# Output projection of a segment recurrence: four column groups of 160 columns against two chunks on two groups of 320 columns each

## The chip, the cores and the metric

The kernel runs on one core of one Trainium2 chip. A core has a TensorE (PE in the profile; its weight loads are PEld), a VectorE (DVE), a ScalarE (ACT), a GpSimd (POOL), and a SyncE (SP) that in this kernel only issues transfers. The metric is the device time of one execution in microseconds.

## What is computed

Four layers run one after the other on 2048 tokens of width 640: A, B, A, B, each added to its input and each fed with a layer-normed copy of it. Layer A is the one that the change touches. Cut to what matters:

```python
# x: 2048 x 640, 32 heads of 192, segments of 32 tokens, a memory of 8 rows
mem = mem0
for s in range(64):
    h = concat([mem, x[32*s : 32*s+32]])             # 40 x 640
    q, k, v = h @ Wq, h @ Wk, h @ Wv                 # each 40 x 6144
    p = softmax(where(mask, q @ k.T * scale, -1e9))  # per head
    o = (p @ v) @ Wo                                 # 6144 -> 640
    mem = o[:8]                                      # feeds the next segment
    outs.append(o[8:])
```

The first 8 rows of a segment's output are the first 8 rows of the next segment's input. So the 64 segments of a layer A form a chain, and two layers A make 128 segments. Layer B is a linear attention whose work is not a chain; the diff leaves it alone.

## The kernel before

**Stages.** A layer A first projects everything that does not depend on the memory (`A_pre`: the last 8 token rows of every segment, written to DRAM as `kqb` and `vb`). Then `A_chain` walks the segments with the remaining 32 rows (8 memory rows, 24 token rows). The order of instructions in `A_chain` is written out by hand (`tc.manual_schedule()`), one order per engine, as the program emits them.

**Rounds.** The 6144 features are cut into four rounds of 1536, taken forwards in even segments and backwards in odd ones (`rounds`). Here n = 0 to 3 counts the rounds in the order in which they are taken. For each round there are three projections of 20 matmuls (Q, K, V: five pieces of the 640 inputs, each on four column groups of 32 output partitions, 384 columns wide), the scores, the exponential (`weigh`), the sums, the product with V (`attend`), the scaling by the reciprocal into the tile OT (`scale_out`), and the output projection `wo_round`. Rounds overlap: the Q and K of the next round are projected between the scores and the product of this one. The order in the middle of a segment is Q(n+1), sums, attend, scores(n), K(n+1), V(n), `wo_round` of the round before. At the end three `wo_round` calls stand close together, with V(3), sums, attend and scores between and before them.

**wo_round.** A round's OT is 12 chunks of 128 features by 32 rows. For each chunk, four matmuls use the same stationary chunk; column group g gets output columns 160g to 160g+159. All 12 chunks of all four rounds are added up in one PSUM tile, `W`, of 128 partitions by 160 columns: 48 matmuls with 48 weight loads per round, 192 of each per segment.

**From W to the next segment.** After the last `wo_round`, `fill(SEG_FILL)` puts 27 one-column weight loads on PE. VectorE transposes W in two parts (L1161) and casts 8 columns of each block into `hT` (L1162), the transposed input of the next segment; its 24 token rows were put there before by `hx_transpose` (L895) from `xr`. Then PE projects Q of the next segment, first the pieces b = 2, 3, 4, then 0, 1. ScalarE evicts Q (`raw`, L955) and after it copies W to `io` (`keep_rows`, L902), from where POOL stores it to DRAM (`store_rows`, L906).

**The extra rows.** The 8 rows that `A_pre` prepared enter by POOL copies: `next_kq` copies them into QT and KT (L916 to L919) and issues the next load of `kqb` (L910); `place_v` copies rows of V (L930) and issues the next (L926). Their attention output leaves the same way: `store_tail` copies 96 columns of OT to `otb` (L1027) and issues a transfer of it to DRAM (L1028). `otb`, OT, `io`, `raw` and `rc` are single buffers: each new write waits until the last reader, or the transfer, is done. `io` holds the rows that are stored and then the rows that are loaded, so the load of `xr` (L890) waits for the landing of the store.

**POOL's order in one segment.** `store_tail` of the last round of the segment before; `store_rows`; `next_kq(0)`; the load of `xr`; `next_kq(1)`; `store_tail` of round 0; `place_v`; `next_kq(2)`; `store_tail` of round 1; `next_kq(3)`; `store_tail` of round 2; `place_v`. The four copies into `otb` are called copy(0) to copy(3) below, after their rounds.

**Weights.** Three of five pieces of one round of Wq, Wk and Wv and one round of Wo do not fit in SBUF; SP loads them anew in every segment into slots (9 loads' worth of 384 KB and 6 of 320 KB, in all about 5.4 MB), as PE frees the slots.

Of the kernel before, what the change touches and what calls it, by code (L numbers as in the profile page):

```python
# [8 lines left out]
P = 128  # L9
BF16 = mybir.dt.bfloat16  # L10
F32 = mybir.dt.float32
ACT = mybir.ActivationFunctionType
ALU = mybir.AluOpType
# [5 lines left out]
LN_EPS = 1e-5  # L19

FILL = {0: 86, 2: 78}
SEG_FILL = 27

LATE = 64512
ARENA = 202752
# [90 lines left out]
class Kernel:  # L116
# [746 lines left out]
    def A_chain(self, xn_dram, at_dram, li, load_slot, piece, load_wo, late_wo, wo_mid, wo_end, low):  # L863
        nc, tc, KC, NSEG = self.nc, self.tc, self.KC, self.NSEG
        scale = float(self.Dh) ** -0.5
        NR = 4
        with tc.tile_pool(name=f"A{li}_ch", reuse_waits="tile", bufs=1) as sp, \
# [6 lines left out]
            OT = sp.tile([P, 6, 80], BF16, name="OT")  # L874
# [4 lines left out]
            def rounds(s):  # L879
                return range(NR) if s % 2 == 0 else range(NR - 1, -1, -1)  # L880

            def load_rows(s):
                io = sp.tile([P, 160], BF16, name="xr", tag="io")
                if s == 0:
                    for g in range(4):
                        c = slice(160 * g, 160 * g + 160)
                        nc.gpsimd.dma_start(out=io[32 * g:32 * g + 8, :], in_=self.A_mem0[:, c])
                        nc.gpsimd.dma_start(out=io[32 * g + 8:32 * g + 32, :], in_=xn_dram[0:24, c])
                else:
                    nc.gpsimd.dma_start(out=io[:, :],  # L890
                                        in_=xn_dram[32 * s - 8:32 * s + 24, :].rearrange("t (g c) -> g t c", g=4))
                return io
# [4 lines left out]
            def new_hT():  # L897
                return sp.tile([P, KC, 32], BF16, name="hT", tag="hT")

            def keep_rows(W):  # L900
                io = sp.tile([P, 160], BF16, name="orow", tag="io")
                nc.scalar.activation(out=io[:, :], in_=W[:, 0:160], func=ACT.Copy)  # L902
                return io

            def store_rows(s, io):
# [2 lines left out]
            def load_kqb(s, r):  # L908
                kqb = sp.tile([P, 192], BF16, name="kqb", tag="kqb", bufs=2)
                nc.gpsimd.dma_start(out=kqb[:], in_=self.kqb_d[s, :, r, :])  # L910
                return kqb
# [46 lines left out]
            def to_rows(raw, m, r=0):  # L958
                if m == "K":
                    nc.vector.transpose(out=KT[:, :, 0:64], in_=raw.rearrange("p (c j) -> p c j", j=64))  # L960
                else:
                    rv = raw.rearrange("p (x i j) -> p x i j", i=3, j=64)
                    q = 16 * (r % 2)
                    nc.vector.transpose(out=QT[:, :, 0:4:3, q:q + 64], in_=rv[:, :, 0:3:2, :])  # L964
                    nc.vector.transpose(out=QT[0:64, :, 1, q:q + 64], in_=rv[0:64, :, 1, :])
                    nc.vector.transpose(out=QT[64:P, :, 2, q:q + 64], in_=rv[64:P, :, 1, :])
# [63 lines left out]
            def wo_round(W, r, first, last):  # L1030
                m0 = 16 * (r % 2)
                w = wo_end[:, :] if r in (0, 3) else wo_mid[:, 7680 * (r - 1):7680 * r]
                for i in range(12):
                    G, c = (i // 4, i % 4) if i < 8 else (i % 4 // 2, 4 + i % 2)
                    for g in range(4):
                        nc.tensor.matmul(W[32 * g:32 * g + 32, 0:160], lhsT=OT[:, c, m0 + 32 * G:m0 + 32 * G + 32],  # L1036
                                         rhs=w[:, 640 * i + 160 * g:640 * i + 160 * g + 160], start=(first and i == 0),
                                         stop=(last and i == 11), tile_position=(0, 32 * g), skip_group_check=True)

            def fill(n):  # L1040

# [5 lines left out]
            def next_kq(s, n):  # L1047

                at = NR * s + n + 1
                if at < len(turns):  # L1050
                    extra_kq(kqs.pop(0), turns[at][1] % 2)
                    if at + 2 < len(turns):
                        kqs.append(load_kqb(*turns[at + 2]))

            xr = load_rows(0)
# [8 lines left out]
            hT = new_hT()  # L1064
            hx_transpose(hT, xr)
            W = None
            for s in range(NSEG):
                order = rounds(s)
                L = NR - 1

                def q_or_k(m, n):
                    ps = pqp.tile([P, 512], F32, name="ps_qk", tag="qk")
                    project(hT, ps, m, n, s)
                    return to_raw(ps, m == "K" and n == 0)

                def values(n, pool, tag):
                    pv = pool.tile([P, 512], F32, name="ps_v", tag=tag)
                    project(hT, pv, "V", n, s)
                    return pv

                raw = q_or_k("Q", 0)
                if s > 0:
                    io = keep_rows(W)
                to_rows(raw, "Q", order[0])
                if s == 0:
                    fill(FILL[li])
                to_rows(q_or_k("K", 0), "K")
                if s == 0:
                    late_wo(2)
                if s > 0:  # L1090
                    store_rows(s - 1, io)
                W = pop.tile([P, 512], F32, name="ps_w", tag="w")
                raw = q_or_k("Q", 1)
                pv = values(0, pop, "v")
                v_rows(pv, 0, "s")
                v_rows(pv, 1, "s")
                S = scores(order[0])
                to_rows(raw, "Q", order[1])
                next_kq(s, 0)
                E = weigh(S)  # L1100
                to_rows(q_or_k("K", 1), "K")
                if s + 1 < NSEG:
                    xr = load_rows(s + 1)
                for n in range(1, L):
                    raw = q_or_k("Q", n + 1)
                    sums(S, E)
                    O = attend(E)
                    if n == 2:
                        place_v()
                    S1 = scores(order[n])  # L1110
                    rc = reciprocals(S)
                    E = weigh(S1)
                    S = S1
                    to_rows(raw, "Q", order[n + 1])
                    next_kq(s, n)
                    if n == L - 1:
                        to_rows(q_or_k("K", n + 1), "K")
                        scale_out(O, rc)
                    else:
                        rawk = q_or_k("K", n + 1)  # L1120
                        scale_out(O, rc)
                        to_rows(rawk, "K")
                    store_tail(s, order[n - 1])
                    pv = values(n, pop, "v")
                    v_rows(pv, 0, "s")
                    v_rows(pv, 1, "s")
                    if n < L - 1:
                        wo_round(W, order[n - 1], n == 1, False)
                        if n == 1:
                            load_wo(order[L])  # L1130
                            if s == NSEG - 1:
                                load_wo(3, low[:, 0:7680])
                pv = values(L, pqp, "qk")
                sums(S, E)
                O = attend(E)
                S1 = scores(order[L])
                next_kq(s, L)
                rc = reciprocals(S)
                E = weigh(S1)
                v_rows(pv, 1, "v")  # L1140
                v_rows(pv, 0, "s")
                wo_round(W, order[L - 2], False, False)
                sums(S1, E)
                O1 = attend(E)
                if s + 1 < NSEG:
                    hT = new_hT()
                    hx_transpose(hT, xr)
                scale_out(O, rc)
                store_tail(s, order[L - 1])
                if s + 1 < NSEG:  # L1150
                    place_v()
                wo_round(W, order[L - 1], False, False)
                rc = reciprocals(S1)
                scale_out(O1, rc)
                wo_round(W, order[L], False, True)
                store_tail(s, order[L])
                fill(SEG_FILL)
                if s + 1 < NSEG:
                    wt = sp.tile([P, KC, 32], F32, name="wt", tag="raw")
                    for b0, b1 in ((2, 5), (0, 2)):  # L1160
                        nc.vector.transpose(out=wt[:, b0:b1, :], in_=W[:, 0:160].rearrange("p (j b) -> p b j", b=KC)[:, b0:b1, :])  # L1161
                        nc.vector.tensor_copy(out=hT[:, b0:b1, 0:8], in_=wt[:, b0:b1, 0:8])  # L1162
            store_rows(NSEG - 1, keep_rows(W))

    def post_steps(self, ops):
# [69 lines left out]
```

## Time and profile before

| what | value |
|---|---|
| three runs | 4068.06, 4073.5, 4086.9 us (median 4073.5) |
| the profiled execution: time, span | 4067.7 us, 4066.0 us |
| mean granted TensorE clock | 0.937 |
| PE matmul busy, PEld busy | 3463.6 us (85%), 2357.2 us (58%) |
| DVE, ACT, POOL busy | 2025.3, 1939.6, 1959.6 us |
| instructions for PE in the trace | 142,876 |
| HBM read and written | 853.72 MB, 73.40 MB |
| segment to segment, mean of 124 (start of L1161 to start of L1161) | 24.03 us |

The two chains of segments take the stretches from about 214 to 1705 us and from about 2248 to 3737 us, some three quarters of the time. A row of the profile's groups gives line, engine, operation, output and inputs, shape and count, then the busy time in us, the mean of one in ns, and the idle time of the engine just before it with what ended that idle time. "issue" is time in which an engine waited for nothing that the profile shows. The matmul's end is modelled, so the distance between the starts of matmuls is a better measure of pace than their length.

### The profile page before, as it was taken

To read this page: it belongs to the slowest core of one execution; us is meant where nothing else is said; L and a number is where in the kernel's file an instruction comes from. 1 tells how busy PE (TensorE), PEld (TensorE's weight loads), DVE (VectorE), ACT (ScalarE), POOL (GpSimd) and SP (SyncE) were. 2 spreads that over 40 slices of the span, in tenths; PEclk is the share of its full clock that TensorE was granted. 3 is DMA by queue.
4 is the path that set the end of the run, shared out by engine and by line. 5 is a ranking of instruction groups with operands and counts; after the bars stand their busy time and mean duration, and the time that the engine had idled before them with its cause. 6 is when DMAs were issued, how large, how long until landed. Compare 5 with 4: busy or idle time off the path is not lost.

```text
span 4066.0 us, 167638 instructions
## 1 busy us (share of the span) xinstructions
PE 3463.6 (85%) x69290; PEld 2357.2 (58%) x72926; DVE 2025.3 (50%) x5432; ACT 1939.6 (48%) x4389; POOL 1959.6 (48%) x4871
## 2 busy tenths in 40 slices
PE   9988888888888888889899888888888888888898
PEld 6755555555555555555377555555555555555553
DVE  5444445445444555446633444554454544544465
ACT  2344455545545455536433444554454545545363
POOL 3455555555555555530333555555555555555300
PEclk9999999999999999989899999999999999999899
DMA  9977777777777777750377777777777777777400
GB/s 304 315 253 252 246 257 261 253 240 254 257 254 250 246 258 262 264 158 1 133 248 235 265 241 248 264 261 242 243 260 252 260 241 249 262 261 261 153 1 27
DMA packets 531754, 934.60 MB, mean 230 GB/s; under 512 B 145458, under 2 KB 295690, under 8 KB 531002
## 3 DMA queue, kind: packets, MB, share of 16 engines
q1 hardware_dynamic: 428858, 818.87, 58.5%
q0 software_dynamic: 68480, 91.75, 7.4%
q10 hardware_dynamic: 33664, 13.24, 1.3%
q8 instruction: 558, 9.14, 0.9%
q14 instruction: 194, 1.59, 0.1%
HBM read 853.72 MB, written 73.40 MB: 228 GB/s over the span
## 4 chain that ended last, share of the span: by engine, by line
PE 48%; DMA 17%; issue 12%; POOL 7%; DVE 6%; PEld 6%; ACT 3%; POOLq 0%; SPq 0%; DVEq 0%; ACTq 0%
PE ps_qk L947 20%; DMA otb<-otb 13%; PE ps_v L947 5%; PE ps_w L1036 4%; PE ps_pre L825 3%; PE ps_s L985 3%; PEld L1036 2%; PEld L1043 2%; PE ps_o L1010 2%; DVE OT L1022 2%; PE ps_qk L391 2%; PE ps_s L996 2%; POOL otb L1027 2%; PE ps_s L980 1%; DVE OT L1018 1%
## 5 line engine op out<-in xcount | busy, mean ns | idle before, releaser
L947 PE MATMUL ps_qk<-arena,hT 128*32 128x384 bf16 x20480 | 1092.8, 352 | 186.1 <-issue 104.0
L947 PEld LDWEIGHTS <-hT 128*32 128x32 bf16 x30720 | 839.0, 101 | 626.1 <-issue 257.0
L955 ACT ACTIVATE raw<-ps_qk 128x384 bf16<-128x384 f32 x1024 | 503.0, 491 | 1287.6 <-PE ps_qk L947 1135.8
L1036 PE MATMUL ps_w<-arena,OT 128*32 128x160 bf16 x24576 | 572.9, 247 | 159.0 <-DVE OT L1018 150.8
L1036 PEld LDWEIGHTS <-OT 128*32 128x32 bf16 x24576 | 454.0, 102 | 254.1 <-DVE OT L1018 221.2
L964 DVE STREAM_TRANSPOSE QT<-raw 128x256 bf16<-128x256 bf16 x512 | 228.0, 445 | 705.9 <-PE ps_s L985 467.1
L947 PE MATMUL ps_v<-arena,hT 128*32 128x384 bf16 x10240 | 509.3, 327 | 14.0 <-DMA arena<-in_A_Wv_dram 13.8
L972 ACT ACTIVATE Vp<-ps_v 64x384 bf16<-64x384 f32 x896 | 433.5, 484 | 96.8 <-PE ps_v L947 76.4
L960 DVE STREAM_TRANSPOSE KT<-raw 128x384 bf16<-128x384 bf16 x512 | 296.1, 578 | 321.2 <-ACT raw L955 314.8
L1018 DVE TENSOR_TENSOR OT<-ps_o,rc 128x320 bf16<-128x320 f32 x512 | 251.5, 491 | 359.5 <-POOL otb L1027 259.8
L1010 PE MATMUL ps_o<-E,Vp 96*128 96x80 bf16 x4096 | 259.0, 202 | 143.3 <-issue 143.0
L910 POOL DMA_DIRECT2D kqb<-kqb x512 | 288.2, 563 | 163.8 <-POOL KT L919 146.7
L1028 POOL DMA_DIRECT2D otb<-otb x512 | 281.2, 549 | 169.4 <-POOL otb L1027 148.3
L1010 PEld LDWEIGHTS <-Vp 96*128 96x128 bf16 x4096 | 222.9, 99 | 187.1 <-DVE OT L1022 136.5
L1022 DVE TENSOR_TENSOR OT<-ps_o,rc 64x160 bf16<-64x160 f32 x1024 | 324.2, 317 | 13.8
L1027 POOL COPY otb<-OT 128x96 bf16<-128x96 bf16 x512 | 135.6, 265 | 324.5 <-DMA otb<-otb 191.0
L930 POOL COPY Vp<-Vp 32x896 bf16<-32x896 bf16 x256 | 237.1, 926 | 77.8 <-PE ps_o L1010 58.6
L1002 ACT ACTIVATE rc<-ps_s 128x320 f32<-128x320 f32 x512 | 224.0, 437 | 77.6 <-DVE OT L1022 64.9
L1001 ACT ACTIVATE ps_s<-ps_s 128x320 f32<-128x320 f32 x512 | 218.6, 427 | 76.4 <-PE ps_s L996 69.9
L985 PE MATMUL ps_s<-QT,KT 128*96 128x80 bf16 (+1 forms) x3072 | 246.1, 217 | 7.8 <-POOL KT L919 3.4
L985 PEld LDWEIGHTS <-KT 128*96 128x96 bf16 x3072 | 222.1, 125 | 39.2 <-issue 28.3
L916 POOL COPY QT<-kqb 128x64 bf16<-128x64 bf16 x512 | 124.2, 242 | 225.9 <-PE ps_s L985 219.3
(149 smaller groups left out, 4744.4 us busy)
## 6 DMA issues: line engine op xcount, KB each, us to landing
arena<-wo_rows SPq DMA_DIRECT2D x792, 320.0 KB, 6.8
arena<-in_A_Wq_dram SPq DMA_DIRECT2D x427, 384.0 KB, 4.6
arena<-in_A_Wv_dram SPq DMA_DIRECT2D x427, 384.0 KB, 6.3
arena<-in_A_Wk_dram SPq DMA_DIRECT2D x768, 192.0 KB, 5.0
kqb<-kqb POOLq DMA_DIRECT2D x512, 48.0 KB, 5.1
arena<-in_A_Wk_dram SPq DMA_DIRECT2D x43, 384.0 KB, 6.9
vb<-arena POOLq DMA_DIRECT2D x128, 112.0 KB, 5.8
Vp<-vb POOLq DMA_DIRECT2D x256, 56.0 KB, 4.8
```

What stands on the lines that cost most here:

```text
L910: nc.gpsimd.dma_start(out=kqb[:], in_=self.kqb_d[s, :, r, :])
L930: nc.gpsimd.tensor_copy(out=Vs[64:96, :], in_=Vs[96:P, :])
L947: nc.tensor.matmul(ps[32 * g:32 * g + 32, 0:384], lhsT=hT[:, b, :], rhs=rhs, start=(i == 0), stop=(i == KC - 1), tile_position=(0, 32 * g) ...
L955: nc.scalar.activation(out=raw, in_=ps[:, 0:384], func=ACT.Copy)
L960: nc.vector.transpose(out=KT[:, :, 0:64], in_=raw.rearrange("p (c j) -> p c j", j=64))
L972: nc.scalar.activation(out=o, in_=i, func=ACT.Copy)
L985: nc.tensor.matmul(S[0:96, c0:c0 + 80 * (q1 - q0)], lhsT=KT[:, 3 * x + i, :], rhs=QT[:, x, q0:q1, :], start=False, stop=(x == 1 and i == 2 ...
L1010: nc.tensor.matmul(O[:, 80 * c:80 * c + 80], lhsT=Vs[0:96, 448 * x + k:448 * x + k + 128], rhs=E[0:96, 160 * x + 80 * e:160 * x + 80 * e + ...
L1018: nc.vector.tensor_tensor(out=OT[:, 0:4, :], in0=ov[:, 0:4, :], in1=rc[:, :].rearrange("p (c q) -> p c q", q=80), op=ALU.mult)
L1022: nc.vector.tensor_tensor(out=OT[h, 4:6, :], in0=ov[h, 4:6, :], in1=rv[h, :, e, :], op=ALU.mult)
L1028: nc.gpsimd.dma_start(out=self.otb_d[s, :, 96 * r:96 * r + 96], in_=ob[:, :])
L1036: nc.tensor.matmul(W[32 * g:32 * g + 32, 0:160], lhsT=OT[:, c, m0 + 32 * G:m0 + 32 * G + 32], rhs=w[:, 640 * i + 160 * g:640 * i + 160 * g ...
```

## The change

`wo_round` takes two chunks at a time. Column groups 0 and 1 work on chunk j, groups 2 and 3 on chunk j+1; each matmul is 320 columns wide (two strips of 160, by an access pattern over the weights), so that partitions 0 to 63 of W collect the even chunks and 64 to 127 the odd ones, over 320 columns. A round is 24 matmuls of 320 columns in place of 48 of 160. W then holds two halves that must be added: for `hT` the transposes cover both strips, and four additions of 64 partitions take the place of two casts; for the stored rows ScalarE copies each half to the other partitions (`half`), and VectorE adds. `keep_rows` is emitted before the Q projection's eviction, not after it. The load of `xr` moves behind `next_kq(1)`. The 27 one-column weight loads go.

```diff
-SEG_FILL = 27
+SEG_FILL = 0
@@ keep_rows
+                half = sp.tile([P, 160], F32, name="half", tag="raw")
                 io = sp.tile([P, 160], BF16, name="orow", tag="io")
-                nc.scalar.activation(out=io[:, :], in_=W[:, 0:160], func=ACT.Copy)
+                for h in range(2):
+                    a, b = slice(64 * h, 64 * h + 64), slice(64 - 64 * h, 128 - 64 * h)
+                    nc.scalar.activation(out=half[a, :], in_=W[b, 160 * h:160 * h + 160], func=ACT.Copy)
+                for h in range(2):
+                    a = slice(64 * h, 64 * h + 64)
+                    nc.vector.tensor_tensor(out=io[a, :], in0=W[a, 160 * h:160 * h + 160], in1=half[a, :], op=ALU.add)
@@ wo_round
-                for i in range(12):
-                    G, c = (i // 4, i % 4) if i < 8 else (i % 4 // 2, 4 + i % 2)
+                for j in range(0, 12, 2):
                     for g in range(4):
-                        nc.tensor.matmul(W[32 * g:32 * g + 32, 0:160], lhsT=OT[:, c, m0 + 32 * G:m0 + 32 * G + 32],
-                                         rhs=w[:, 640 * i + 160 * g:640 * i + 160 * g + 160], start=(first and i == 0),
-                                         stop=(last and i == 11), tile_position=(0, 32 * g), skip_group_check=True)
+                        i = j + g // 2
+                        G, c = (i // 4, i % 4) if i < 8 else (i % 4 // 2, 4 + i % 2)
+                        wi = w[:, 640 * i:640 * i + 640].rearrange("p (h e c) -> p e h c", h=2, e=2)
+                        nc.tensor.matmul(W[32 * g:32 * g + 32, 0:320], lhsT=OT[:, c, m0 + 32 * G:m0 + 32 * G + 32],
+                                         rhs=wi[:, g % 2], start=(first and j == 0), stop=(last and j == 10),
+                                         tile_position=(0, 32 * g), skip_group_check=True)
@@ A_chain, start of a segment
-                raw = q_or_k("Q", 0)
                 if s > 0:
                     io = keep_rows(W)
+                raw = q_or_k("Q", 0)
...
                 to_rows(q_or_k("K", 1), "K")
-                if s + 1 < NSEG:
-                    xr = load_rows(s + 1)
                 for n in range(1, L):
...
                     next_kq(s, n)
+                    if n == 1 and s + 1 < NSEG:
+                        xr = load_rows(s + 1)
@@ A_chain, end of a segment
-                    wt = sp.tile([P, KC, 32], F32, name="wt", tag="raw")
+                    wt = sp.tile([P, 2, KC, 32], F32, name="wt", tag="rc")
+                    wv = W[:, 0:320].rearrange("p (h j b) -> p h b j", h=2, b=KC)
                     for b0, b1 in ((2, 5), (0, 2)):
-                        nc.vector.transpose(out=wt[:, b0:b1, :], in_=W[:, 0:160].rearrange("p (j b) -> p b j", b=KC)[:, b0:b1, :])
-                        nc.vector.tensor_copy(out=hT[:, b0:b1, 0:8], in_=wt[:, b0:b1, 0:8])
+                        nc.vector.transpose(out=wt[:, :, b0:b1, :], in_=wv[:, :, b0:b1, :])
+                        for h in range(2):
+                            a, b = slice(64 * h, 64 * h + 64), slice(64 - 64 * h, 128 - 64 * h)
+                            nc.vector.tensor_tensor(out=hT[a, b0:b1, 0:8], in0=wt[a, h, b0:b1, 0:8], in1=wt[b, h, b0:b1, 0:8],
+                                                    op=ALU.add)
```

PE's instructions per segment go from 1019 to 800, besides five semaphore waits that stand in both.

## The prediction

> **What bounds the kernel now.** I read the page first, then the waits, then the chain and the timeline of some segments, and at last the same events averaged over 124 segments ("phase" below: us after the start of the first transpose L1161, which follows the end of W; a segment lasts 24.03).
>
> ```profile
> span 4066.0 us, 167638 instructions
> ...
> q8 instruction: 558, 9.14, 0.9%
> ...
> PE 48%; DMA 17%; issue 12%; POOL 7%; DVE 6%; PEld 6%; ACT 3%; POOLq 0%; SPq 0%; DVEq 0%; ACTq 0%
> ...
> L1036 PE MATMUL ps_w<-arena,OT 128*32 128x160 bf16 x24576 | 572.9, 247 | 159.0 <-DVE OT L1018 150.8
> ```
>
> PE has less than half of the chain. 17% is transfers, nearly all of `otb`, and 12% is "issue". Queue q8 fetches instructions: 142,876 PE instructions in 558 packets are 256 a packet.
>
> ```profile
> DVE OT L1018 <- POOL otb L1027: 259.8, 114, 5.1
> PE ps_o L1010 <- issue: 143.0, 121, 2.0
> PE ps_qk L947 <- issue: 104.0, 117, 2.2
> POOL xr L890 <- DMA attn<-orow: 93.0, 73, 3.3
> ```
>
> The second and third rows are one thing. Counted along PE, both gaps stand at the same place modulo 256 in every segment (1019 instructions and 5 semaphore waits make 1024, four packets), and each ends 2.3 to 2.5 us after a q8 packet started. They are waits for instructions: one in K(3), at phase 14, 1.1 us in the mean, one in the last `attend`, at phase 20, 1.3 us. The other two boundaries of a segment cost 0.0 and 0.2. The packet itself starts 3.5 to 3.7 us after the boundary before while weights stream, and about 1 us after it when they don't: while weights stream, 256 instructions can't take less than some 6.2 us.
>
> ```profile
> 1023.16 5.95 DMA otb<-otb
> ...
> 1029.24 0.26 POOL otb L1027
> ...
> 1029.79 2.96 DMA otb<-otb
> ...
> 1032.87 0.27 POOL otb L1027
> ...
> 1035.69 3.55 PE ps_qk L947 x54
> ...
> 1048.32 1.14 issue
> ```
>
> The chain shows the other bound: copy(0), its transfer, copy(1), its transfer, copy(2), then `scale_out` and the last `wo_round`. Mean phases: copy(0) 11.33, landing 17.2; copy(1) 17.7, landing 21.5; copy(2) 21.7; W ends at 24.0. copy(2) is bound by the landing in 100 of 122 segments. That landing comes 0.8 us (median) after the last weight packet, which ends at 20.4 (19.8 to 21.3): the weights, at 330 to 370 GB/s from phase 2.5 to 18, hold it up.
>
> **The change part by part**, per segment; 126 segment ends.
>
> *Matmuls.* In a round the 48 matmuls start over 0.792 us, 16.9 ns apart. [...] PE is paced by columns, 12 x 160 = 6 x 320, so I take 0.
>
> *Instructions.* PE loses 192 for the matmuls and 27 in the fill: 805 a segment, 3.14 packets. [...] The rows show 247 us of stalls, so removing all would be 2.0 us a segment if they were on the path. The boundaries now drift by 37 instructions a segment. The densest stretch (K(2), V(1), `wo_round`, Q(3) to V(3): 320 instructions in some 7.1 us) takes 5.7 us for 256, against 6.2: I allow 0 to 0.5 us in about half of the segments, with slack behind it.
>
> *What the stalls were worth.* K(3)'s 1.1 us: `scale_out` of round 2 ended at 17.17 and now at 16.1. But copy(1) also waits for copy(0)'s landing, 17.21. The moved `xr` load is why that comes earlier: POOL's four copies of `next_kq(1)` start 1.02 us after the scores are done, 0.07 without the load before them. The load (0.71 us of POOL, no gap) then stands between the `kqb` issue and copy(0): scores at 8.30 + 0.07 + 1.01 copies + 0.30 + 0.57 issue + 0.71 = 10.96, so copy(0) gains 0.3, and its landing with it (16.9; its transfer is now right behind `xr`'s, which could cost up to 0.4). Its other neighbours on the queue only change places; the store of 8.27 has landed long before. copy(1): 17.7 to 17.1. copy(1)'s transfer lands earlier by 0.42 of what it is issued earlier (fit over the segments), by all of it if the weights let it, by nothing if not: 0 to 0.6, value 0.45. The last `attend`'s 1.3 us ends in front of `scale_out`'s wait for copy(2); it counts only where the second last `wo_round` came later than copy(2) (44 of 122): 0.13 mean. Sum -0.58.
>
> *W to Q.*
>
> ```profile
> 1035.14 0.28 DVE L1161 STREAM_TRANSPOSE wt<-ps_w 128x96 f32<-128x96 f32 x1 [0.90 <-PE L1043]
> 1035.46 0.17 DVE L1162 CAST hT<-wt 128x24 bf16<-128x24 f32 x1
> 1035.55 0.23 DVE L1161 STREAM_TRANSPOSE wt<-ps_w 128x64 f32<-128x64 f32 x1
> ```
>
> The transpose of 96 columns takes 283 ns, of 64 231: 52 per 32, so 192 take 0.44, +0.16. Two additions in place of the cast, the second starting some 0.1 later: +0.10 (as casts cost 0.19, 64x160 additions 0.32). The second part ends 0.54 after Q starts and is needed after three pieces, 0.48: +0.04. Sum +0.30, straight on the path, and the weight stream starts that much later too.
>
> *keep_rows.* Two ScalarE copies (128x160 took 298 ns) run in its idle time before Q's eviction; two additions of 317 ns (L1022's) on DVE, after `hT`'s, end about 2.0 after W. Q's eviction now waits for them through the buffer of `raw`, and K's, Q(1)'s stand behind it on ACT; it started at 1.59 at the earliest, so with +0.30 at most 0.1 is exposed, and KT had 0.25 in hand before PE's scores. 0; if that cover is gone, 0.1. `wt` in the buffer of `rc` only follows DVE's own reads and K(0)'s eviction later: 0.
>
> *The fill.* It ran in PE's wait for `hT` (0.40 of 0.67 us): 0 by itself. Its part in the clock is next.
>
> *The clock.* The trace grants half clock in pieces of 3.413 us or two of them. Such a piece follows a window of 3.413 us in which matmuls were busy for less than about half (33 drops: 0.17 to 0.55; windows without: tenth percentile 0.68).
>
> ```profile
> 1029.00:1032.40 3.40, 1.38 (x53) 1.00 (x52) 1.04 (x3) 0.44 (x1) 2.19 (x7) 1.00 0.09 29
> 1032.40:1035.80 3.40, 1.50 (x52) 1.53 (x83) 1.65 (x6) 0.00 (x0) 2.26 (x5) 0.76 0.08 22
> 1035.80:1039.20 3.40, 3.40 (x64) 1.87 (x64) 1.34 (x5) 1.18 (x3) 1.51 (x3) 0.73 0.63 197
> ```
>
> 71 of 124 segment ends have one. Those pieces are not idle: the last `wo_round` then takes 1.5 us, not 1.0, and segments whose front was slow lasted 0.4 longer. Now the 1.3 us of the last `attend` move behind the second last `wo_round`, so idle time lies in one stretch of up to 2.9 us. The range is -0.1 (the waits shrink) to +0.8 (nearly every end slow, two pieces each). I take +0.05, because 1.0 of the moved idle time was already in the same window.
>
> Sum: -0.58 + 0.30 + 0.05 = -0.23 us a segment, x 126 = -29 us. The profiled execution took 4067.7 (2 us around its span); the median is 4073.5, 6 above it. 4073.5 - 29 = 4045.
>
> **The rivals.** *The landing follows copy(1) fully and the drops grow rarer:* -0.58 becomes -0.9, the clock gives 0.1 or more back: -0.7 us, about 3985. For it: issue is 12% of the chain. Against: the last weight packet doesn't depend on K(3).
>
> *The change only trades one wait for another:* the landing stays at the last weight packet, 0.13 is left against 0.30: +0.15, 4075 to 4095.
>
> *Slower by the clock:* the merged idle stretch drops the clock at nearly every segment end, and often for two pieces, which the Q, K and V projections then run in. It decides once the window before the last `wo_round` is busy for less than half in over nine of ten ends. Price: last `wo_round` +0.2, front +0.5 (Q(2)'s phase runs from 8.7 to 10.6 with the clock): +0.75 instead of 0.05, sum +0.45, or 4130; with part of it hidden under the weights 4100. For it: the removed fill and stalls; against: copy(1) earlier shortens the wait.
>
> *The change doesn't do what it says:* if the weights' two-strip pattern slows the 320 columns, `wo_round` lasts over 0.85 us; the K projections' own stepped pattern runs at V's pace, so this is unlikely.
>
> **How the numbers follow.** A run tells about 0.5%, 20 us, from nothing. Likeliest case (0.45): 4010 to 4070. Fully following (0.25): 3940 to 4010. Trade (0.12) around 4085; slower by the clock and others (0.18): 4095 to 4130. Faster by over 0.5% (under 4053): 0.25 + 0.32 of 0.45 = 0.57. Within: 0.13 + 0.10 = 0.23. Slower: 0.02 + 0.18 = 0.20. Range 3945 to 4108.
>
> **What the profile after would show.** Right: `wo_round` starts spread over 0.8 us still; PE's "issue" rows for L947 and L1010 fall from 247 to under 60 us; `xr` no longer waits for `attn`; copy(1) near phase 17.3, W-to-Q 0.3 longer; DVE's wait for `otb` stays or grows. Wrong: if "issue" stays, the instruction fetch is misread; if the granted clock falls below 0.92, the clock rival has won; if the last weight packet moves earlier by more than 0.3, something I hold fixed moved.

## The result, and the profile after

| | before | after |
|---|---|---|
| median, lowest and highest of 20 runs, us | 4078.49 (4062.24 to 4098.35) | 4086.76 (4065.58 to 4106.55) |
| ratio after to before, 95% interval | | 1.0019 (1.0001 to 1.0038) |
| the profiled execution, us | 4067.7 | 4097.91 |
| mean granted TensorE clock in it | 0.937 | 0.914 |
| segment to segment, us (mean of 124) | 24.03 | 24.23 |

The forecast was 29 us faster. What came is 8 us slower by the medians, 0.2%, within the 0.5% that a measurement of this kernel tells from nothing. Phases below are mean times after the first transpose of W (L1161 before, L1170 after) in the profiled executions. These two lie 11 us under and 11 us over their medians, so the segments in the table show 0.20 us of loss where the medians make it 0.06. With the change, lines move: `wo_round` is L1044, the projections are L953, `half` is L905, the addition of the stored rows L908, the addition into `hT` L1173, the copies into `otb` L1033. The page after:

```profile
span 4096.2 us, 140384 instructions
...
PE 3500.1 (85%) x57018; PEld 2106.2 (51%) x57182; DVE 2181.2 (53%) x5940; ACT 1981.7 (48%) x4517; POOL 1957.4 (48%) x4871
...
q8 instruction: 448, 7.34, 0.7%
...
L1044 PE MATMUL ps_w<-arena,OT 128*32 128x320 bf16 x12288 | 565.6, 320 | 351.0 <-DVE OT L1024 341.8
...
L905 ACT ACTIVATE half<-ps_w 64x160 f32<-64x160 f32 x256 | 76.3, 298 | 666.4 <-DVE wt L1170 489.7
```

27,000 instructions are gone, and instruction packets fall from 558 to 448. `wo_round` is as busy as before, 565.6 us against 572.9, with half the matmuls. But its idle time in front has gone from 159.0 to 351.0 us. DVE has 156 us more to do. (The chain on this page covers only a few per cent of the span, so it isn't read.) In the waits, PE's "issue" rows for the K projection and `attend` are gone; counted between starts, such gaps fall from 312 us in 242 events to 5.1 in 8. These lines (total us, times, longest) are new or stayed:

```profile
ACT half L905 <- DVE wt L1170: 489.7, 88, 7.3
...
DVE OT L1024 <- POOL otb L1033: 345.9, 159, 4.2
...
PEld L953 <- DVE hT L1173: 210.0, 252, 1.6
...
POOL attn L912 <- DVE orow L908: 117.1, 113, 1.9
...
PE ps_qk L953 <- DVE hT L1173: 113.0, 126, 1.0
```

DVE waits for `otb` at the end of the round more than before, 345.9 us against 259.8. PE's loads now wait for `hT` twice at every segment end (252 times in 126). The timeline of one end shows both, and what `half` does to Q:

```profile
1013.09 0.38 DVE L1170 STREAM_TRANSPOSE wt<-ps_w 128x192 f32<-128x192 f32 x1 [0.56 <-PE ps_w L1044]
1013.50 0.37 DVE L1173 TENSOR_TENSOR hT<-wt 64x24 bf16<-64x24 f32 x2
...
1013.90 0.32 DVE L1170 STREAM_TRANSPOSE wt<-ps_w 128x128 f32<-128x128 f32 x1
...
1013.93 2.06 PE L953 MATMUL ps_qk<-arena,hT 128*32 128x384 bf16 x40 [0.89 <-DVE hT L1173]
...
1014.31 0.61 ACT L905 ACTIVATE half<-ps_w 64x160 f32<-64x160 f32 x2 [4.80 <-PE ps_qk L953]
...
1014.66 1.09 PEld L953 LDWEIGHTS <-hT 128*32 128x32 bf16 x29 [0.45 <-DVE hT L1173]
1014.95 0.66 DVE L908 TENSOR_TENSOR orow<-ps_w,half 64x160 bf16<-64x160 f32 x2 [0.34 <-ACT half L905]
1015.72 0.87 ACT L961 ACTIVATE raw<-ps_qk 128x384 bf16<-128x384 f32 x2 [0.81 <-PE ps_qk L953]
...
1016.27 1.00 PE L953 MATMUL ps_qk<-arena,hT 128*32 128x384 bf16 x20 [0.28 <-ACT raw L961]
```

Q starts 0.84 after the first transpose; before it was 0.55. Then the weight loads stop for 0.45, until the second part of `hT` is added. ScalarE does not begin `half` in its idle time right after W, as assumed, but at 1014.31, 0.09 after the second transpose has ended (1014.22). Two copies, then DVE's two additions up to 1015.61, and only then does ScalarE evict Q, at 1015.72, 2.6 after the first transpose. Q(1) needs the PSUM buffer that this frees, and its matmuls wait for it at 1016.27.

The other visible thing is the clock. These are four successive stretches of 3.41 us at the next segment end (columns: length, then busy us and instructions of PE, PEld, DVE, ACT and POOL, granted clock, DMA share, GB/s):

```profile
1028.22:1031.64 3.42, 3.42 (x77) 2.30 (x69) 3.16 (x9) 2.59 (x7) 1.84 (x6) 1.00 1.07 380
1031.64:1035.05 3.41, 0.52 (x16) 0.12 (x8) 0.31 (x2) 0.44 (x1) 1.43 (x6) 1.00 0.30 93
1035.05:1038.46 3.41, 2.27 (x32) 1.08 (x36) 1.95 (x8) 0.09 (x1) 2.74 (x5) 0.50 0.11 29
1038.46:1041.87 3.41, 3.41 (x52) 1.60 (x44) 1.77 (x7) 1.44 (x4) 0.77 (x2) 0.50 0.68 191
```

In the second, PE is busy for 0.52 of 3.41 us; the third and fourth run at half clock, with the last `wo_round` in the third and most of the Q projections in the fourth. In the 124 segments half clock takes 546 us, before 375.

So three suspects for the lost gain: the additions at the segment end, the clock, and that the stalls were never worth what they lasted. In mean phases:

| | before | after |
|---|---|---|
| Q(1) evicted, start | 4.06 | 5.12 |
| copy(0) | 11.23 | 11.96 |
| K(3) evicted, start | 14.94 | 15.08 |
| copy(1) | 17.66 | 18.12 |
| copy(2) | 21.65 | 22.00 |
| end of W | 24.03 | 24.23 |

(The prediction's 11.33 and 17.7 for copy(0) and copy(1) are a little high: in a few segments copy(3) falls on the other side of the transpose, which shifts a count by place. Here the copies are counted by their order.) The front is 1.06 later. At K(3) only 0.14 of that is left, for K(3) has lost its stall of about 1 us. Then copy(1) is 0.46 and copy(2) 0.35 later.

### The profile page after: what moved, and what is told of

Same layout as the page of the kernel before. It is cut to its first block, busy times and chain, and to the rows that moved or that the text cites. A ratio compares the mean times of both kernels' runs of the same rounds, so it can differ in the third digit from the quotient of the medians.

```text
span 4096.2 us, 140384 instructions
## 1 busy us (share of the span) xinstructions
PE 3500.1 (85%) x57018; PEld 2106.2 (51%) x57182; DVE 2181.2 (53%) x5940; ACT 1981.7 (48%) x4517; POOL 1957.4 (48%) x4871
## 5 line engine op out<-in xcount | busy, mean ns | idle before, releaser
L953 PE MATMUL ps_qk<-arena,hT 128*32 128x384 bf16 x20480 | 1140.4, 371 | 126.1 <-DVE hT L1173 113.0
L953 PEld LDWEIGHTS <-hT 128*32 128x32 bf16 x30720 | 828.8, 104 | 734.3 <-DVE hT L1173 210.0
L1044 PE MATMUL ps_w<-arena,OT 128*32 128x320 bf16 x12288 | 565.6, 320 | 351.0 <-DVE OT L1024 341.8
L1044 PEld LDWEIGHTS <-OT 128*32 128x32 bf16 x12288 | 266.8, 100 | 570.9 <-DVE OT L1024 435.7
L953 PE MATMUL ps_v<-arena,hT 128*32 128x384 bf16 x10240 | 492.6, 328 | 16.0 <-DMA arena<-in_A_Wv_dram 13.5
L1024 DVE TENSOR_TENSOR OT<-ps_o,rc 128x320 bf16<-128x320 f32 x512 | 251.5, 491 | 378.2 <-POOL otb L1033 345.9
L905 ACT ACTIVATE half<-ps_w 64x160 f32<-64x160 f32 x256 | 76.3, 298 | 666.4 <-DVE wt L1170 489.7
L1033 POOL COPY otb<-OT 128x96 bf16<-128x96 bf16 x512 | 135.8, 265 | 259.9 <-DMA otb<-otb 205.5
L1016 PE MATMUL ps_o<-E,Vp 96*128 96x80 bf16 x4096 | 242.8, 203 | 0.9 <-POOL Vp L936 0.4
```

The source lines that it names most:

```text
L953: nc.tensor.matmul(ps[32 * g:32 * g + 32, 0:384], lhsT=hT[:, b, :], rhs=rhs, start=(i == 0), stop=(i == KC - 1), tile_position=(0, 32 * g) ...
L1016: nc.tensor.matmul(O[:, 80 * c:80 * c + 80], lhsT=Vs[0:96, 448 * x + k:448 * x + k + 128], rhs=E[0:96, 160 * x + 80 * e:160 * x + 80 * e + ...
L1024: nc.vector.tensor_tensor(out=OT[:, 0:4, :], in0=ov[:, 0:4, :], in1=rc[:, :].rearrange("p (c q) -> p c q", q=80), op=ALU.mult)
L1044: nc.tensor.matmul(W[32 * g:32 * g + 32, 0:320], lhsT=OT[:, c, m0 + 32 * G:m0 + 32 * G + 32], rhs=wi[:, g % 2], start=(first and j == 0), ...
```

## The experiments

Each ratio is to the kernel before on the same chip, with its 95% interval; e1 to e4, e5 to e8 and e9 to e12 ran on one chip each. The clock, the segment and the half clock (in the 124 segments) are those of the profiled execution.

| run | what it is | ratio | clock | segment, us | half clock, us |
|---|---|---|---|---|---|
| after | the change | 1.0019 (1.0001 to 1.0038) | 0.914 | 24.23 | 546 |
| e1 | `half` in a buffer of its own | 1.0043 (1.0021 to 1.0064) | 0.916 | 24.15 | 534 |
| e2 | no adding of halves | 0.9941 (0.9919 to 0.9962) | 0.925 | 23.74 | 454 |
| e3 | after, 8 extra matmuls | 0.9896 (0.9867 to 0.9924) | 0.971 | 23.61 | 72 |
| e4 | before, 8 extra matmuls | 0.9954 (0.9939 to 0.9969) | 0.979 | 23.72 | 31 |
| e5 | e3 and e1 | 0.9915 (0.9886 to 0.9945) | 0.974 | 23.65 | 85 |
| e6 | e5, `xr` at its old place | 0.9936 (0.9913 to 0.9958) | 0.974 | 23.72 | 61 |
| e7 | e2, 8 extra matmuls | 0.9776 (0.9746 to 0.9805) | 0.971 | 23.23 | 82 |
| e8 | after, with the fill | 1.0076 (1.0049 to 1.0104) | 0.915 | 24.23 | 549 |
| e9 | e4, 1024 instructions a segment | 0.9882 (0.9851 to 0.9913) | 0.980 | 23.68 | 24 |
| e10 | before, 5 extra, 1024 | 0.9798 (0.9762 to 0.9834) | 0.981 | 23.13 | 17 |
| e11 | before, 3 extra, 1024 | 0.9787 (0.9763 to 0.9812) | 0.976 | 23.27 | 51 |
| e12 | after, 5 extra | 0.9948 (0.9926 to 0.9969) | 0.953 | 23.84 | 236 |

**e1_half_own.** `half` leaves the buffer of `raw`, so that Q's eviction needn't wait for the additions.

```diff
-                half = sp.tile([P, 160], F32, name="half", tag="raw")
+                half = sp.tile([P, 160], F32, name="half", tag="E")
```

> The changed kernel, with the tile of the shifted half in the buffer of E and no longer in that of the evicted Q, so that Q's eviction does not wait for the two additions of the stored rows. Theory 1 (the gain of the removed instruction stalls is eaten between the end of W and Q(1): longer transposes and additions, then the eviction of Q behind the stored rows, which holds back the projection of Q(1)): the eviction of Q starts near phase 2.3 instead of 2.71, Q(2) about 0.4 earlier than 8.82, and the time is 0.3 us a segment below the changed kernel's: near 4050, ratio to before 0.99. Theory 2 (the half clock eats it): the eviction is hidden by the slow front anyway, ratio 1.00. Theory 3 (the transfer of the second otb copy is pinned to the last weight packet): Q starts when it did, so the weights start when they did, and the ratio stays 1.00.

Q's eviction starts at 2.14 at the earliest in place of 2.64, and the tenth percentile of Q(1)'s eviction moves from 4.27 to 3.81: the chain through `half` is 0.46 long. The mean of Q(1) moves by only 0.09 (5.12 to 5.03), and the time does not fall. Half clock was the suspect for covering this term; e5 tests that.

**e2_no_halves.** The second half of W is left out: each part has one transpose and one cast of the first 160 columns again, and `keep_rows` is one copy after the Q eviction, as before. The 320-column matmuls, the 27 missing loads and the moved `xr` stay.

```diff
-                wt = sp.tile([P, 2, KC, 32], F32, name="wt", tag="rc")
+                wt = sp.tile([P, KC, 32], F32, name="wt", tag="raw")
...
-                        nc.vector.transpose(out=wt[:, :, b0:b1, :], in_=wv[:, :, b0:b1, :])
...
+                        nc.vector.transpose(out=wt[:, b0:b1, :], in_=W[:, 0:160].rearrange("p (j b) -> p b j", b=KC)[:, b0:b1, :])
+                        nc.vector.tensor_copy(out=hT[:, b0:b1, 0:8], in_=wt[:, b0:b1, 0:8])
```

> The changed kernel's 24 wide matmuls and its xr load and no fill, but the end of a segment as before: one transpose of 160 columns, two casts, one copy to the stored rows after Q's eviction. The other half of W is left out, so that this tells what the fewer instructions are worth without the work of adding halves. Theory 1: stalls gone and nothing paid for it: front phases as before (Q(2) evicted near 7.7 to 7.9), time 0.5 to 0.9 us a segment below before's, 3965 to 4015, ratio 0.973 to 0.985. Theory 2: the front is as slow as the changed kernel's through the clock, ratio above 0.99. Theory 3: second otb landing at phase 21.5 as before, ratio 0.995 to 1.0.

0.6% faster than before, so the rest of the change is a gain as the kernels stand, of a third of the size forecast: 0.19 us a segment (1% is 0.32 us a segment). The adding takes back 1.0019/0.9941, 0.8% or 0.25 us.

**e3_warm_after, e4_warm_before.** Eight matmuls of 512 columns into a spare PSUM buffer, in front of the last `wo_round`, keep PE busy there. Their results aren't used.

```diff
+            def warm(n):
+                pw = pop.tile([P, 512], F32, name="ps_v", tag="v")
+                for _ in range(n):
+                    nc.tensor.matmul(pw[:, :], lhsT=self.ident[:, :], rhs=wo_mid[:, 0:512], start=True, stop=True,
+                                     skip_group_check=True)
...
+                warm(8)
                 wo_round(W, order[L], False, True)
```

> The changed kernel with eight matmuls of 512 columns on constant operands into a spare PSUM bank, between the second last and the last Wo round, where PE waits some 3 us for the last scale_out. Theory 2: half clock in the two chains falls from 550 us to under 150, the last Wo round from 1.5 to 1.0 us, Q(1) is evicted 0.4 or more earlier; time 0.4 to 0.8 us a segment lower, 3985 to 4040. Theory 1: the half clock falls just the same but the front is bound by VectorE and the eviction of Q: at most 0.2 us a segment, 4060 or more. Theory 3: the last Wo round is shorter by 0.3 us and the front counts little: 4040 to 4060.

> The kernel before with the same eight matmuls at the same place. Its idle time there is shorter (the last attend's instruction stall lies ahead of it), so the eight matmuls may delay the last Wo round in some segments. Theory 2: half clock falls from 380 us to under 150 and the time by 0.2 to 0.4 us a segment, to 4030 to 4055. Theories 1 and 3: what is won in the clock is lost in delayed Wo rounds, ratio 0.995 to 1.005.

The clock rises in both (0.914 to 0.971 and 0.937 to 0.979), and half clock all but vanishes from the chains (546 to 72 us and 375 to 31 us). The two gains, 1.2% for the changed kernel and 0.5% for the one before, made it look as if the clock had eaten the change's gain. That reading was wrong: in the kernel before the eight matmuls did two more things, as e9 to e11 show.

**e5_half_own_warm, e6_xr_early.** e5 is e1's edit with the eight matmuls. e6 is e5 with the load of `xr` back in front of the rounds:

```diff
                 to_rows(q_or_k("K", 1), "K")
+                if s + 1 < NSEG:
+                    xr = load_rows(s + 1)
                 for n in range(1, L):
...
-                    if n == 1 and s + 1 < NSEG:
-                        xr = load_rows(s + 1)
```

> The changed kernel with both: the shifted half in the buffer of E, and the eight constant matmuls before the last Wo round. Theory 1 and 2 together (the chain from W over the eviction of Q to Q(1) is worth some 0.45 us a segment once the clock is full; at half clock it was hidden by the slow projections): Q(1) evicted near phase 3.8 instead of 4.3, time 20 to 55 us below the run with the matmuls alone, ratio to before 0.976 to 0.985. Rival (the later transfers of otb and the weights decide, not the front): within 10 us of the run with the matmuls alone, ratio 0.988 to 0.992.

> The same kernel as the run before in this set, with the load of the next rows back at its old place, ahead of the second set of POOL copies. My prediction had copy(0) 0.3 us later that way: 5 to 25 us slower than its neighbour. If the load's place does not count: within 5 us. If copy(0)'s transfer suffers from the load's transfer right ahead of it: faster by up to 20 us.

In e5 Q(1) is 0.4 earlier than in e3 and copy(1) 0.2; copy(2) stays (21.66 and 21.69), and so does the time. So it is not half clock that covers the chain through `half`: a gain in the front is gone again when copy(1)'s transfer has landed. In e6 copy(0) is 0.7 later (10.95 to 11.66) and copy(1) 0.56 (17.38 to 17.94), but copy(1)'s transfer lands when it did, at 21.54 and 21.55. The last weight packet ends at 20.70 and 20.59. The move of `xr` does what was forecast for copy(0) and more, and next to nothing of it reaches the end of the segment. The intervals of e5 and e6 overlap.

**e7_no_halves_warm.** e2 with the eight matmuls; the second half of W is left out again.

> The kernel that leaves out the second half of W (end of a segment as before), with the eight constant matmuls. It gives the worth of the fewer instructions when neither the clock nor the halves take it away: with Q(1) evicted at 3.3 and no instruction stalls, 3.3 + (7.76 - 4.07) = about 0.9 us a segment below the changed kernel with the matmuls if the front is on the path: 3930 to 3970, ratio 0.965 to 0.975. If the last weight packet decides: 3990 or more, ratio above 0.98.

At full clock the adding costs 0.9896/0.9776, 1.2% or 0.39 us a segment. It delays Q, and with it the weights: between phases 2 and 3 the weight queue moves 229 GB/s in e7 and 139 in e3, and its last packet ends at 20.32 and 20.54. copy(1)'s landing and copy(2) are 0.37 and 0.38 later in e3, as the end of W is.

**e8_fill27_after.** The changed kernel with the old fill (`SEG_FILL = 27`).

> The changed kernel with the 27 one-column weight loads put back. If their absence is what lost the clock (theory 2 in its narrow form): granted clock back from 0.914 to 0.93 or more, 20 to 40 us faster. If the clock is lost through the long wait before the last Wo round, which lies ahead of the fill: clock and time as the changed kernel's, 4080 to 4092.

Clock 0.915 and 549 us of half clock: the fill did not keep the clock up, and its removal didn't lower it. Nor does the fill make the kernel faster: its ratio is even 0.6% above the changed kernel's, with intervals that do not overlap. The phases of the two profiled executions show no cause for that (both segments 24.23), and it stays open.

**e9_warm_before_1024.** In the trace of before, the stalls in K(3) and in the last `attend` stand 256 and 768 instructions of PE apart in turn (109 times each), so with 1024 a segment they come at the same two places. In e4, the 16 added instructions (eight loads and eight matmuls) make it 1040, and the stalls come at other places from segment to segment. e9 takes 16 from the fill, so that a segment has 1024 again.

```diff
-SEG_FILL = 27
+SEG_FILL = 11
...
+                warm(8)
```

> The kernel before with the eight extra matmuls of 512 columns in front of the last wo_round, and the fill cut from 27 to 11 one-column weight loads, so that a segment has 1024 PE instructions and waits again and the block boundaries stay where they stand in the kernel before: in K(3) and in the last attend. Both stalls should be back (about 1.1 and 1.3 us a segment, some 290 us over the run, against about 91 us in the version with 27), the clock should stay near 0.975. Theory (the stalls were worth what the forecast gave them, 0.58 us a segment, and half clock cost the kernel before little): the time is close to the kernel before, ratio 0.992 to 1.000, and clearly longer than the version with 27 (0.9954) if that one's relief of stalls was what made it faster. Rival (half clock was what cost the kernel before, and the stalls stood beside other work): as fast as the version with 27 or faster, 0.990 to 0.996, for with the stalls in fixed places nothing else is changed.

Both stalls are back in full, 129.1 us in the K projection and 176.5 in `attend` (e4: 21.1 and 8.3). The time is not longer but 0.7% shorter than e4's, under both ranges. So putting the stalls back in their two places did not lengthen the time; and there was still something in the way:

```profile
1069.71 0.34 PE L1010 MATMUL ps_o<-E,Vp 96*128 96x80 bf16 x5 [1.21 <-issue]
...
1070.93 1.90 PE L1043 MATMUL ps_v<-arena,ident 128*128 128x512 bf16 x8
...
1071.52 0.49 DVE L1018 TENSOR_TENSOR OT<-ps_o,rc 128x320 bf16<-128x320 f32 x1 [2.42 <-POOL otb L1027]
...
1072.76 1.01 PE L1036 MATMUL ps_w<-arena,OT 128*32 128x160 bf16 x48
```

In this timeline of e9 the first line is the stall in the last `attend` (1.21). The eight matmuls come after it and run for 1.90. The first part of OT was ready at 1072.01 (1071.52 + 0.49), but `wo_round` starts at 1072.76, when they are through. In the mean the last `wo_round` starts 1.05 after the start of its `scale_out` in e9, 0.56 in e3. That half microsecond a segment is the price of the extra matmuls themselves.

**e10_warm5_before, e11_warm3_before, e12_warm5_after.** Fewer of them; the kernel before keeps its 1024 with a fill of 17 and 21.

```diff
-SEG_FILL = 27
+SEG_FILL = 21
...
+                warm(3)
```

> The kernel before with five extra matmuls of 512 columns in front of the last wo_round and 17 fill loads (1024 PE instructions and waits a segment, so both instruction stalls stay in their places). With eight, the last wo_round began 0.47 us later than its OT allowed, because the extra matmuls stood in front of it until then; five are 0.64 us shorter and should be gone in time. Theory now (the stalls in K(3) and the last attend stand beside other work, and half clock is what the kernel before pays for): the clock stays at or above 0.965, the segment comes to about 23.2 us, ratio 0.972 to 0.980, as fast as the changed kernel without its halves (0.9776). Rival (the stalls cost what the forecast gave them, 0.58 us a segment): not under 0.985, for they are all still there. A third outcome: five are too few, the clock falls under 0.955 and the time lies between.

> As with five, but three extra matmuls and 21 fill loads. They cover 0.6 us of a wait of 2.2 us. If a window of 3.413 us needs only somewhat over half of busy matmuls, three are nearly enough: clock 0.96 or more and ratio 0.973 to 0.985. If not, the clock is between 0.94 and 0.96 and the ratio 0.985 to 0.995.

> The changed kernel with five extra matmuls in front of the last wo_round in place of eight; beside the kernel before with five, it is the change at full clock with nothing in the way of the last wo_round. With eight they ended 0.95 us ahead of it in the mean, so taking three away frees nothing: if the clock holds (0.965 or more), ratio 0.987 to 0.993, and slower than the kernel before with five by some 1.0 to 1.6% in the theory (the halves cost 0.4 us a segment and the stalls were worth nothing); equal or faster than it in the rival. If five are too few for its wait of 3.1 to 3.5 us, the clock falls to 0.94 to 0.96 and the ratio to 0.99 to 1.0.

The kernel before with three or five extra matmuls is 2.1% and 2.0% faster than without, with every instruction stall in it. This is e11, its waits first:

```profile
core 0: 3972.7 us, clock 0.976
```
```profile
DVE OT L1018 <- POOL otb L1027: 334.7, 131, 4.5
...
POOL otb L1027 <- DMA otb<-otb: 253.9, 170, 4.5
...
PE ps_o L1010 <- issue: 151.1, 118, 2.0
...
POOL otb L1027 <- DVE OT L1022: 105.9, 95, 3.5
...
PE ps_qk L947 <- issue: 88.5, 113, 2.0
```

In e7, without the stalls, POOL waits less for `scale_out` (L1022) and more for the landing, and DVE waits longer for POOL:

```profile
DVE OT L1018 <- POOL otb L1027: 378.9, 162, 4.2
...
POOL otb L1027 <- DMA otb<-otb: 306.0, 221, 5.2
...
POOL otb L1027 <- DVE OT L1022: 11.6, 9, 4.9
```

And the timeline of a segment end in e11:

```profile
1050.70 0.34 PE L1010 MATMUL ps_o<-E,Vp 96*128 96x80 bf16 x5 [0.63 <-issue]
...
1050.97 1.01 PE L1036 MATMUL ps_w<-arena,OT 128*32 128x160 bf16 x48
...
1051.91 0.82 PE L1043 MATMUL ps_v<-arena,ident 128*128 128x512 bf16 x2
...
1052.99 0.26 POOL L1027 COPY otb<-OT 128x96 bf16<-128x96 bf16 x1 [2.30 <-DMA otb<-otb]
1053.29 0.49 DVE L1018 TENSOR_TENSOR OT<-ps_o,rc 128x320 bf16<-128x320 f32 x1 [2.63 <-POOL otb L1027]
...
1053.84 1.04 PE L1036 MATMUL ps_w<-arena,OT 128*32 128x160 bf16 x48 [1.10 <-DVE OT L1018]
```

The stall of 0.63 in `attend` stands right in front of a stretch in which POOL waits 2.30 for the landing and DVE 2.63 for POOL. The extra matmuls (two of the three are in the records) fill part of PE's wait and are gone 1.1 before OT comes. e11's 0.9787 and e7's 0.9776 are the same within their intervals: at full clock the change without its adding brings nothing measurable over the kernel before. With its adding (e3 against e11) it is 0.9896/0.9787, 1.1% slower; the two intervals make that uncertain by about 0.4%. In e12 five matmuls are too few, since without the stall the wait in front of the last `wo_round` is longer: half clock still takes 236 us.

Beside e7, which leaves part of the work out, e11 is the fastest kernel here: 3978.67 us against 4066.53 for the kernel before on its chip, and by the two ratios 2.3% under the changed kernel. (e10's segment in the table is from its fastest execution, 3957 us; its median is 3990.17, and the intervals of e10 and e11 overlap.)

## Why the prediction was wrong

The sum was -0.58 (stalls) + 0.30 (W to Q) + 0 (`keep_rows`, fill, matmuls) + 0.05 (clock) = -0.23 us a segment. By the medians:

| step, us a segment | forecast | as the kernels stand | at full clock |
|---|---|---|---|
| the change without the adding | -0.58 | -0.19 (e2 to before) | -0.04 (e7 to e11) |
| the adding and its order | +0.30 | +0.25 (after to e2) | +0.39 (e3 to e7) |
| sum | -0.28 | +0.06 | +0.35 |

The forecast's +0.05 for the clock is part of the middle column, where the clocks differ.

*"What the stalls were worth" failed, and with it the sign.* Its first half was right: fewer instructions, no stall, and the `scale_out` ahead of copy(1) (the prediction calls it round 2's) ends 0.57 earlier at full clock, at 15.72 in e7 and 16.29 in e11. Two steps behind it failed. The first is "copy(0) gains 0.3, and its landing with it (16.9)": the landing of copy(0) is at 16.80 in e7 and at 16.35 in e11, so later, not earlier. In e7 copy(1) starts within 0.3 of it in 119 of 124 segments, in e11 in 79, and copy(1) stands at 16.95 and 16.67: the wait changed its name, from `scale_out` to the landing. (Its transfer takes 5.70 from issue to landing in e7, 5.39 in e11; why isn't shown. The load of `xr` right ahead of it explains at most a part: with it moved away, 5.51 in e6 against 5.66 in e5.) As the kernels stand it is the same: `scale_out` ends 0.53 earlier in e2 than before, the landing comes 0.28 later, and copy(1) moves by 0.04.

The second is that copy(1)'s landing follows copy(1), by "0 to 0.6, value 0.45". Its 0.42 was a fit over the segments of one kernel; where an experiment moved copy(1), less came through: 0.56 became 0.01 at the landing in e5 against e6, and 1.20 became 0.27 in e9 against e4. The last weight packet ends at 20.32 in e7 and 20.29 in e11, the landing comes 0.8 behind it in both (21.13 and 21.09), and copy(2) follows at 21.28 and 21.24. So even an earlier copy(1) would have met the next wait. Of the rivals, "the change only trades one wait for another" had just this, and its time (4075 to 4095) holds the result, though its 0.13 and 0.30 were not what was measured.

The last `attend`'s stall, priced at 0.13, stands in front of a wait of over 2 us in the timeline of e11. From copy(2) to the last `wo_round` it takes 0.96 before and 0.84 in e2, so there the 0.13 came in; at full clock it is 0.92 in e11 and 0.85 in e7.

With the adding and half clock, copy(0) came at 11.96, not 10.96, its landing at 17.88 in place of 17.18, and copy(1) went up by 0.46 where -0.6 was forecast.

The stalls are real, 1.0 to 1.4 us each in the mean in every run with 1024 instructions, so here PE does wait for its instructions. Yet their worth, 0.04 us a segment (e7 to e11), was nearer to 0 than to the 0.58 made from the rows (247 us of stalls). What hides the stall from the segment's time is the transfer chain beside it: copy(1)'s landing is at 21.13 in e7 and at 21.09 in e11.

That PE is paced by columns, and with it the 0 for the matmuls, was the author's estimate. No run varies the width alone; what the traces show is this: a V projection before (20 matmuls of 384 columns), a `wo_round` before (48 of 160) and one after (24 of 320), each 1920 columns on every column group, start over 0.66, 0.79 and 0.72 us (medians). From its first start to the transpose of W the last `wo_round` takes 1.09 us (median) after and 1.10 before.

*"W to Q" was right, "the second part" was not.* W to Q took 0.29 more, of 0.26 forecast for transpose and additions. Waiting for the second part of `hT` was put at +0.04 because three pieces of PE's work were to cover it; the timeline shows the additions end 0.67 after Q starts, and weight loads that stop for 0.45. From Q's first matmul to the 13th, where the second part is needed, it is 0.51 in e11 and 0.75 in e3: it cost 0.24.

*`keep_rows` at 0 failed in the front, and was right at the end by luck.* "If that cover is gone, 0.1": e1 and e5 measured 0.46 in the front. The premise that ScalarE copies "in its idle time" had the start wrong: `half` starts after the second transpose, 1.2 after the first, not right after W, and DVE's additions end 2.53 after it, not "about 2.0". Yet taking the 0.46 away gained no time (e5 against e3), for the landing behind it stayed. Together the three make the front 1.01 later at full clock (Q(1)'s eviction at 4.28 in e3, 3.27 in e11, medians), of which 0.39 is left at the end of the segment. In all 124 segments `half` starts 0.09 to 0.37 after the second transpose has ended; why wasn't tried. It reads W, which the transpose also reads.

*The clock was right in its direction, and wrong in what counted.* The idle stretches did merge, the clock fell under 0.92 (0.914), half clock grew from 375 to 546 us. But the forecast asked only what the change would add to it. What it cost already was never priced: taking it away is worth 2.1% in the kernel before (0.69 us a segment) and 1.2% in the changed one (0.40). In phases, before against e11: Q(1) from 4.06 to 3.32, copy(2) from 21.65 to 21.24, and the last `wo_round` starts 1.42 and 1.11 ahead of the segment's end; 0.41 and 0.31 make 0.72 of the 0.76 between the two segments. The forecast had named both places ("the last `wo_round` then takes 1.5 us, not 1.0"). The rival "slower by the clock" has its mechanism, but not its price: it added 0.75 us a segment for it, where nearly all half clock in the changed kernel costs 0.40.

*Confirmed:* the fill is worth no gain (e8), though whether it costs something is open; the matmuls at 0 (the busy time of `wo_round` moved by 7 us in the whole run); `xr` no longer waits for `attn`; the gain of copy(0) by the moved load (0.7 between e6 and e5).

*Open:* e4 (0.9954) is 0.7% slower than e9 (0.9882) although its stalls are fewer. Its stalls drift through all places of a segment, 69.8 us of them in `wo_round`, and copy(1) comes 1.2 later than in e9; that drifting stalls find worse places than fixed ones is the likely reason, but no run put a stall in a chosen place.

## What to carry to other kernels

Before pricing the removal of a stall, ask which wait ends next at the same point and when: here one landing took over within the stall's length and a second stood behind it, and nothing that could be measured of 0.57 us came through. Look at the granted clock as a cost of its own, and test it with a few spare matmuls in the wait that lets it fall, as few as hold the clock and gone before the real work is ready. What a change adds where a chain is closed (here from W to the next Q) counts in full at first, so follow every buffer that the first eviction shares.

## What the runs showed of the hardware

- In the trace of before, half clock came in 93 stretches: 41 of 3.413 us, 51 of two, three or four times that, and one of 2.772; all 93 started within 0.001 us of multiples of 3.413 us from each other. In its 124 segments there are 70 drops; in the 3.413 us ahead of a drop matmuls were busy for a median share of 0.41, and never for more than 0.55; of the 691 full-clock windows of that length without a drop behind them only three were under 0.50. The changed kernel has 101 drops, with a median of 0.30. Three matmuls of 512 columns in front of the last `wo_round` removed most of the half clock (375 to 51 us, e11).
- A mean clock of 0.937 looked like a loss of 6% of PE's pace spread over everything; taking most of it away won 2.1%, at two places of a segment.
- Instruction stalls of 303 us in e11, a tenth of its two chains of segments, could go at a worth of 0.04 us a segment (e7; uncertain by about 0.12): transfers landed behind them at their own time.
- More half clock wasn't more cost: taking away 474 of 546 us in the changed kernel won 1.2% (e3), 324 of 375 us in the one before 2.1% (e11).
- A transfer's landing need not follow its issue: 0.56 us at copy(1) became 0.01 at its landing (e5, e6), which comes 0.8 to 1.0 us behind the last weight packet there.
